# The start of a sliding-window attention kernel: x by halves and row tiles, two GpSimd moves less, one copy on ScalarE

## The chip, the cores and the metric

The kernel runs on one core of a Trainium2 chip. A core has five engines that run side by side and meet only at semaphores: TensorE (PE, matmuls; its weight loads are shown apart as PEld), VectorE (DVE), ScalarE (ACT), GpSimd (POOL) and SyncE (SP), which issues most of the DMAs. The metric is the device time of one execution in microseconds, the median of several runs; less is better.

## The reference

Eight sequences of 32 new positions each attend to a window of 2048 cached positions, 32 query heads over 4 key/value heads.

```python
B, Sq, D = 8, 32, 1024;  Hq, Hkv, Sk, Dh = 32, 4, 8192, 128      # bf16
W = min(4096, max(256, Sk // 4))                                 # 2048
q = (x @ wq).reshape(B, Sq, Hq, Dh).transpose(0, 2, 1, 3)
k = repeat(k_cache[:, :, Sk - W:, :], 8, axis=1)                 # v likewise
p = softmax(einsum("bhqd,bhkd->bhqk", q, k) * Dh ** -0.5)
o = einsum("bhqk,bhkd->bhqd", p, v)
return o.transpose(0, 2, 1, 3).reshape(B, Sq, Hq * Dh) @ wo
```

## The kernel before

The work is cut into 32 units, one for each pair of key/value head g and sequence b, in the order g 0 with b 0 to 7, then g 1, and so on. A unit has 256 queries (8 heads of 32 rows) and 2048 keys in 16 tiles of 128. It runs in four chunks of four key tiles. For a chunk PE computes the scores (L504, four matmuls into `s_ps`, from kT and the projected queries QT), ACT takes the exponential into `pT` (L506), and two chunks later PE multiplies `pT` by V (L515, eight matmuls into `o_ps`; V has a column of ones, which gives the softmax's sum). `s_ps` has two buffers, so the scores of a chunk wait for the exp two chunks before. When a unit is through, `finish_unit` on DVE divides and transposes (L444, L448, L450). The order of instructions on every engine is that of the program text (`manual_schedule`), and `side_plan` puts side work into numbered slots, four to a unit: pieces of the query projections of later heads (`q_pieces`, L285), of the output projection (`o_pieces`, L321), and the preparation of some K tiles.

The scores need K transposed (`kT`), and there are three ways to get it:

- Units 0, 1 and 2: K is loaded as it is (`k_raw`, L192, L197), transposed by PE, and copied out of PSUM by DVE (unit 0: L396, L400; units 1 and 2: `k_pieces`, L244, L246).
- The units of the table `V_T` (4, 7, 9, 12 and so on): K is loaded as it is, DVE transposes 32x32 blocks in four pieces (L259, `kb`), and sixteen moves put the blocks in their places (`kTv`). The last number of a unit's entry says how many of the sixteen go to POOL (L270); the others are DVE's (L268). Unit 9 has 12, so DVE has four, and its moves are spread over the slots 26 to 33; the unit's own scores begin in slot 36.
- All others: a transposing DMA (L200).

V is copied into the `va` buffers (L438 on DVE, L436 on POOL for units 1 and 2). Loads are issued by SP in the order of the text; a load waits on SP for its buffer to come free, and everything behind it on SP waits too.

`start` is what comes ahead of unit 0. x is 256 rows in two row tiles of 128. Tile 0 is loaded by SP (L346), tile 1 by ACT's queue (L347), then SP issues the weights of head group 0 (`wq`, L168, four pieces of one chunk, then one of two, and two of one; a chunk is 128 of the 1024 inputs), with the first half of unit 0's K between (L197). Meanwhile PE runs `N_WARM` matmuls on constants (L374). `x_turn` then transposes x with PE: eight chunks times two row tiles, in two halves of four chunks, each half into one PSUM tile; DVE copies the first two chunks of a half into `xT`, ACT the other two. Then `q_mm` projects (L404): for each of the eight chunks, heads 0 to 3 with all 256 rows and heads 4 to 7 with the 128 rows of tile 0 alone. Rows 128 to 255 of heads 4 to 7 come later in `q_late` (L301, slots 0 to 2 for heads 4 and 5, slots 8 to 12 for heads 6 and 7), two heads at a time, and a copy by DVE (L304) puts them into QT, where unit 4 is the first that reads them.

Of the kernel before, what the change touches and what calls it, by code (L numbers as in the profile page):

```python
# [11 lines left out]
BF16 = mybir.dt.bfloat16  # L12
# [3 lines left out]

RL_LIMIT = 1.0e22
RL_MIN = 1.0e-10
N_WARM = 8
VA_ROW = 160  # L20
V_HALVES = 30

# [1 line left out]

V_T = {4: (None, (4, 6, 6, 7), 8, 15, 9),
       7: (4, (18, 18, 19, 20), 20, 27, 12),
       9: (5, (23, 24, 25, 26), 26, 34, 12),
       **{u: (u - 4, range(4 * u - 14, 4 * u - 10), 4 * u - 11, 4 * u - 2, 12) for u in (12, 14, 17, 19, 22, 24, 27, 29)}}
W_AT = (3, 3, 4, 4, 8, 8, 9, 9, 11, 12, 13, 14, 15, 15, 17, 17, 18, 19, 19, 20, 22, 22, 23, 24, 25, 26, 28, 28)

# [78 lines left out]
class Fast:  # L109
# [183 lines left out]
    def q_late(self, h0):  # L293
        nc, P, DC, B = self.nc, self.P, self.DC, self.B
        st = {}

        def piece(i):
            if i == 0:
                st["ps"] = self.ps_m.tile([P, 2, P], FP32, name="ql_ps", tag="m")
            for c in range(DC):  # L300
                nc.tensor.matmul(st["ps"][:, i, :], lhsT=self.wq_t[0, c // (DC // 2)][:, c % (DC // 2), (h0 + i) * P:(h0 + i + 1) * P],  # L301
                                 rhs=self.xT[:, c, P:self.NQ], start=(c == 0 and i == 0), stop=(c == DC - 1), skip_group_check=True)
            if i == 1:
                nc.vector.tensor_copy(out=self.q_view(0)[:, B // 2:, h0:h0 + 2, :].rearrange("p b h s -> p h b s"),  # L304
                                      in_=st["ps"][:, :, :].rearrange("p h (b s) -> p h b s", b=B // 2))
        return [lambda i=i: piece(i) for i in range(2)]

    def o_pieces(self, g, t, cuts=(512, 512), st=None):
# [29 lines left out]
    def start(self):  # L338
        nc, P = self.nc, self.P
        warm = self.ps_s.tile([P, 512], FP32, name="warm_ps", tag="s_ps")  # L340
        one = nc.const_aps.tensor
        x_sb = self.vp.tile([P, self.NT, self.D], BF16, name="x_sb", tag="v")
        xf = self.x.rearrange("b s d -> (b s) d")
        H = self.DC // 2

        nc.sync.dma_start(out=x_sb[:, 0, :], in_=xf[0:P, :])  # L346
        nc.scalar.dma_start(out=x_sb[:, 1, :], in_=xf[P:2 * P, :])  # L347
        wq0 = self.load_wq(0, 0, (1, 1, 1, 1)) + self.load_wq(0, 1, (2, 1, 1))
        for p in wq0[:5]:
            p()  # L350
        self.load_k(0, 0)
        wq0[5]()
        wq0[6]()
        self.load_k(0, 1)
        self.load_v(0, nc.sync)
        self.load_k(1)
        self.weights = []
        for g in range(self.Hkv):
            if g + 1 < self.Hkv:
                self.weights += self.load_wq(g + 1, 0) + self.load_wq(g + 1, 1)  # L360
            if g:
                self.weights += self.load_wo(2 * g - 2) + self.load_wo(2 * g - 1)
        self.weights += self.load_wo(2 * self.Hkv - 2) + self.load_wo(2 * self.Hkv - 1)
        self.load_v(1, nc.sync)
        self.load_k(2)
        self.load_k(4)
        self.load_v(2, nc.sync)
        self.load_unit(3)
        for v in self.va:
            nc.gpsimd.memset(v[:, :, self.Dh:self.VW], 1.0)  # L370
        nc.gpsimd.memset(self.ones_c[:, :], 1.0)
        def warm_up(n):
            for i in range(n):
                nc.tensor.matmul(warm[:, :], lhsT=one(1.0, [P, P], BF16), rhs=one(1.0, [P, 512], BF16), start=True, stop=True)  # L374
        warm_up(N_WARM)


        def x_turn(half, pl, tag):
            ps = pl.tile([P, H, self.NT, P], BF16, name="xT_ps", tag=tag)
            for c in range(H):  # L380
                for t in range(self.NT):
                    nc.tensor.transpose(ps[:, c, t, :], x_sb[:, t, half * H + c:self.D:self.DC], self.ident[:, :])
            for i, copy in ((0, nc.vector.tensor_copy), (1, nc.scalar.copy)):
                c0 = half * H + i * H // 2
                copy(out=self.xT[:, c0:c0 + H // 2, :], in_=ps[:, i * H // 2:(i + 1) * H // 2, :, :].rearrange("p c t s -> p c (t s)"))

        x_turn(0, self.ps_m, "m")
        x_turn(1, self.ps_s, "s_ps")
        qs = [self.ps_o.tile([P, 2, self.NQ], FP32, name="q0_ps", tag="o_ps") for _ in range(2)]
        qs.append(self.ps_m.tile([P, 4, P], FP32, name="q0_ps", tag="m"))  # L390
        KT = self.KT
        tp = None

        def k_turn(half):
            for j in range(half * KT // 2, (half + 1) * KT // 2):
                nc.tensor.transpose(tp[:, j, :], self.k_raw[0][:, j, :], self.ident[:, :])  # L396

        def k_copy(half):
            sl = slice(half * KT // 2, (half + 1) * KT // 2)
            nc.vector.tensor_copy(out=self.kT[0][:, sl, :], in_=tp[:, sl, :])  # L400

        def q_mm(c, h):
            ps, n = (qs[h // 2][:, h % 2, :], self.NQ) if h < 4 else (qs[2][:, h - 4, :], P)
            nc.tensor.matmul(ps, lhsT=self.wq_t[0, c // H][:, c % H, h * P:(h + 1) * P],  # L404
                             rhs=self.xT[:, c, 0:n], start=(c == 0 and h in (0, 2, 4)), stop=(c == self.DC - 1),
                             skip_group_check=True)

        def q_copy(copy, h0, h1, b0, b1):
            ps = qs[h0 // 2] if h0 < 4 else qs[2]
            copy(out=self.q_view(0)[:, b0:b1, h0:h1, :].rearrange("p b h s -> p h b s"),  # L410
                 in_=ps[:, :, b0 * self.Sq:b1 * self.Sq].rearrange("p h (b s) -> p h b s", s=self.Sq))

        for c in range(self.DC):
            if c == self.DC - 2:
                tp = self.ps_s.tile([P, KT, P], BF16, name="kf_ps", tag="s_ps")
                k_turn(0)
                k_copy(0)
            for h in range(self.rep):
                q_mm(c, h)
            if c == 0:  # L420
                warm_sb = self.c1.tile([P, 8], BF16, name="warm_sb")
                nc.vector.tensor_copy(out=warm_sb[:, :], in_=warm[:, 0:8])
        k_turn(1)
        q_copy(nc.scalar.copy, 0, 2, 0, 1)
        q_copy(nc.vector.tensor_copy, 2, 4, 0, 1)
        q_copy(nc.scalar.copy, 4, 8, 0, 1)
        k_copy(1)
        self.va_copy(0)
        q_copy(nc.vector.tensor_copy, 0, 2, 1, self.B)
        q_copy(nc.vector.tensor_copy, 4, 8, 1, self.B // 2)  # L430
        q_copy(nc.vector.tensor_copy, 2, 4, 1, self.B)
# [262 lines left out]
```

## Time and profile before

| | |
|---|---|
| median of 7 runs | 186.35 us (185.36 to 187.9) |
| the profiled execution | 187.34 us, of which the span is 184.6 us |
| PE busy | 178.8 us (97% of the span) |
| PE weight loads | 152.7 us |
| ACT busy | 136.0 us, of it 128.6 in 128 exps of 1027 ns (L506) |
| DVE busy | 123.8 us |
| POOL busy | 90.8 us, of it 86.0 in 129 moves of 667 ns (L270) |
| DVE's moves (L268) | 47 of 430 ns |
| DMA | 51.72 MB, mean 280 GB/s; 512 KB of K or V take about 6 us from issue to landing |
| TensorE clock granted | 0.999 |

The span is what the profiler recorded from the first to the last instruction; the time of an execution includes what lies around it. A group's "idle before" is the time in which its engine did nothing just ahead of it, with the instruction or DMA that ended the wait behind an arrow. PE's groups overlap by their pipelining, so holes are read from the distance of the starts.

### The profile page before, as it was taken

What the parts mean: (1) busy time and instruction counts of PE and PEld (TensorE: products, weight loads), DVE (VectorE), ACT (ScalarE), POOL (GpSimd) and SP (SyncE); (2) the same over time, 40 slices, a digit from 0 to 9 for tenths busy, and PEclk for the clock granted to TensorE, in tenths of its full rate; (3) what the DMA queues carried; (4) which work ended last, traced back from release to release, by engine and by line L of the source; (5) the groups of instructions that cost most, each with busy time, mean ns of one, the idle gap of its engine ahead of it and who ended that gap; (6) DMA issues with size and microseconds to landing.
All of it is one profiled execution on the core that took longest, in us unless ns stands there. A gap on an engine that the chain in (4) does not pass through costs nothing.

```text
span 184.6 us, 5015 instructions
## 1 busy us (share of the span) xinstructions
PE 178.8 (97%) x2026; PEld 152.7 (83%) x2041; DVE 123.8 (67%) x255; ACT 136.0 (74%) x145; POOL 90.8 (49%) x141
## 2 busy tenths in 40 slices
PE   8999999999999999999999999999999999999994
PEld 3899898999998999988767899987878788888843
DVE  0138699689769786486589667767588987554253
ACT  2218788898899888897786687888787788888800
POOL 2002567069891976916917915929805949600000
PEclk9999999999999999999999999999999999999999
DMA  5999999899999999999999999999999999950003
GB/s 194 330 408 404 211 383 373 260 253 253 365 395 237 353 274 289 373 288 375 232 380 335 402 260 286 355 273 354 277 319 221 364 265 361 218 166 0 0 32 89
DMA packets 52953, 51.72 MB, mean 280 GB/s; under 512 B 39744, under 2 KB 40256, under 8 KB 52928
## 3 DMA queue, kind: packets, MB, share of 16 engines
q1 hardware_dynamic: 52352, 50.90, 97.8%
q10 hardware_dynamic: 576, 0.49, 0.9%
q8 instruction: 15, 0.25, 0.5%
q14 instruction: 10, 0.08, 0.1%
HBM read 41.42 MB, written 0.52 MB: 227 GB/s over the span
## 4 chain that ended last, share of the span: by engine, by line
PE 68%; DMA 12%; DVE 10%; POOL 4%; SPq 2%; issue 2%; POOLq 0%
PE o_ps L515 23%; PE s_ps L504 23%; PE op_ps L321 12%; PE q_ps L285 9%; DMA k_raw<-in_k_cache_dram 9%; POOL kTv L270 4%; DMA v_sb<-in_v_cache_dram 4%; DVE kb L259 3%; DVE kTv L268 2%; DVE o_sb L448 1%; SPq L168 1%; DVE va L438 1%; DVE OT L450 1%; SPq L200 1%; DVE kT L246 1%
## 5 line engine op out<-in xcount | busy, mean ns | idle before, releaser
L506 ACT ACTIVATE pT<-s_ps 128x1024 bf16<-128x1024 f32 x128 | 128.6, 1027 | 29.0 <-PE s_ps L504 28.7
L270 POOL TENSOR_SCALAR kTv<-kb 32x512 bf16<-32x512 bf16 x129 | 86.0, 667 | 51.1 <-DVE kb L259 21.1
L515 PE MATMUL o_ps<-va,pT 128*128 128x129 bf16 x1024 | 78.8, 220 | 0.1
L515 PEld LDWEIGHTS <-pT 128*128 128x128 bf16 x1024 | 68.5, 98 | 3.1
L504 PE MATMUL s_ps<-QT,kT 128*128 128x256 bf16 x336 | 50.4, 273 | 0.5 <-ACT pT L506 0.3
L504 PEld LDWEIGHTS <-kT 128*128 128x128 bf16 x336 | 31.8, 98 | 10.3 <-DMA kT<-in_k_cache_dram 0.7
L321 PE MATMUL op_ps<-wo_sb,OT 128*128 128x512 bf16 (+2 forms) x129 | 32.9, 353 | 0.6
L259 DVE STREAM_TRANSPOSE kb<-k_raw 128x512 bf16<-128x512 bf16 x44 | 29.7, 691 | 2.0 <-DMA k_raw<-in_k_cache_dram 1.7
L285 PE MATMUL q_ps<-xT,wq_sb 128*128 128x256 bf16 x192 | 28.3, 273 | 0.0
L438 DVE COPY va<-v_sb 128x2048 bf16<-128x2048 bf16 x30 | 25.3, 843 | 4.4 <-DMA v_sb<-in_v_cache_dram 3.9
L504 PE MATMUL s_ps<-QT,kTv 128*128 128x256 bf16 x176 | 26.4, 272 | 0.9 <-DVE kTv L268 0.5
L444 DVE RECIPROCAL RL_all<-o_ps 128x2 f32<-128x2 f32 x32 | 5.4, 167 | 28.0 <-PE o_ps L515 27.6
L504 PEld LDWEIGHTS <-kTv 128*128 128x128 bf16 x176 | 16.8, 98 | 7.6 <-issue 1.0
L268 DVE COPY kTv<-kb 32x512 bf16<-32x512 bf16 x47 | 20.2, 430 | 1.1
L285 PEld LDWEIGHTS <-wq_sb 128*128 128x128 bf16 x192 | 16.9, 98 | 1.2
L450 DVE STREAM_TRANSPOSE OT<-o_sb 128x256 bf16<-128x256 bf16 x32 | 14.3, 445 | 1.1
L448 DVE TENSOR_TENSOR o_sb<-o_ps,RL_all 128x256 bf16<-128x256 f32 x32 | 13.6, 424 | 1.1
L321 PEld LDWEIGHTS <-OT 128*128 128x128 bf16 x144 | 11.3, 98 | 2.3
L436 POOL TENSOR_SCALAR va<-v_sb 128x2048 bf16<-128x2048 bf16 x2 | 3.8, 1899 | 17.9 <-DMA v_sb<-in_v_cache_dram 17.9
L288 ACT CAST QT<-q_ps 128x512 bf16<-128x512 f32 x12 | 7.0, 580 | 0.2 <-PE q_ps L285 0.2
L328 DVE TENSOR_TENSOR oacc<-op_ps,oacc 128x512 f32<-128x512 f32 x8 | 5.3, 662 | 2.0 <-PE op_ps L321 2.0
L404 PE MATMUL q_ps<-xT,wq_sb 128*128 128x256 bf16 (+1 forms) x64 | 6.2, 254 | 0.2 <-DMA wq_sb<-in_wq_dram 0.2
(34 smaller groups left out, 43.8 us busy)
## 6 DMA issues: line engine op xcount, KB each, us to landing
v_sb<-in_v_cache_dram SPq DMA_DIRECT2D x30, 512.0 KB, 6.6
wo_sb<-in_wo_dram SPq DMA_DIRECT2D x16, 512.0 KB, 6.5
wq_sb<-in_wq_dram SPq DMA_DIRECT2D x13, 512.0 KB, 6.6
k_raw<-in_k_cache_dram SPq DMA_DIRECT2D x13, 512.0 KB, 5.7
wq_sb<-in_wq_dram SPq DMA_DIRECT2D x6, 256.0 KB, 4.8
v_sb<-in_v_cache_dram SPq DMA_DIRECT2D x4, 256.0 KB, 4.8
kT<-in_k_cache_dram SPq DMA_TRANSPOSE x36, 7.0
k_raw<-in_k_cache_dram SPq DMA_DIRECT2D x2, 256.0 KB, 6.5
```

What stands on the lines that cost most here:

```text
L259: nc.vector.transpose(out=st["kb"][:, sl, :], in_=self.k_raw[ui][:, sl, :])
L268: nc.vector.tensor_copy(out=out, in_=in_)
L270: nc.gpsimd.tensor_scalar(out=out, in0=in_, scalar1=1.0, scalar2=1.0, op0=ALU.mult, op1=ALU.mult)
L285: nc.tensor.matmul(st[k][:, hl % 2, :], lhsT=self.wq_t[g, i][:, c % (DC // 2), hl * P:(hl + 1) * P], rhs=self.xT[:, c, :], start=(c == 0 a ...
L288: nc.scalar.copy(out=self.q_view(g)[:, :, 2 * k:2 * k + 2, :].rearrange("p b h s -> p h b s"), in_=st[k][:, :, :].rearrange("p h (b s) -> ...
L321: nc.tensor.matmul(ps[:, 0:w], lhsT=self.OT[:, gq, c, t * P:(t + 1) * P], rhs=self.wo_t[gq][:, c, n0:n0 + w], start=(k == 0), stop=(k == 7))
L438: self.nc.vector.tensor_copy(out=out, in_=in_)
L448: nc.vector.tensor_tensor(out=o_sb[:, :, :, :], in0=o_ps[:, :, 0:Dh].rearrange("p q (i c) -> p q c i", c=4), in1=rl[:, ui * QT_N:(ui + 1) ...
L450: nc.vector.transpose(out=self.OT[:, g * QT_N:(g + 1) * QT_N, :, b * self.Sq:(b + 1) * self.Sq], in_=o_sb[:, :, :, :])
L504: nc.tensor.matmul(s_ps[:, jj, :], lhsT=self.kT[ui][:, c * CJ + jj, :], rhs=q_u, start=True, stop=True)
L506: nc.scalar.activation(out=pT[:, :, :], in_=s_ps[:, :, :], func=ACT.Exp, bias=0.0, scale=self.scale)
L515: nc.tensor.matmul(o_ps[:, qt, 0:self.VW], lhsT=pT[:, jj, qt * P:(qt + 1) * P], rhs=va[:, j, 0:self.VW], start=(j == 0 and qt == 0), stop= ...
```

## The change

Four things change. The load of x tile 0 is cut into two halves by columns, one issued by SP and one by ACT, ahead of ACT's load of tile 1; one warm-up matmul is left out (8 to 7). `x_turn` takes a row tile instead of a half of the chunks: eight transposes of tile 0 into one PSUM tile, eight of tile 1 into the other; DVE copies chunks 0 to 3 of a row tile and ACT chunks 4 to 7, and in chunk 0 the projection takes heads 4 to 7 first. Unit 9 gives 10 moves to POOL instead of 12, and 6 to DVE. The copy of the second `q_late` group (heads 6 and 7) is made by ACT instead of DVE; it stands behind the eleventh exp and ahead of the twelfth.

```diff
--- before.py
+++ after.py
@@ -16,7 +16,7 @@
 
 RL_LIMIT = 1.0e22
 RL_MIN = 1.0e-10
-N_WARM = 8
+N_WARM = 7
 VA_ROW = 160
 V_HALVES = 30
 
@@ -24,7 +24,7 @@
 
 V_T = {4: (None, (4, 6, 6, 7), 8, 15, 9),
        7: (4, (18, 18, 19, 20), 20, 27, 12),
-       9: (5, (23, 24, 25, 26), 26, 34, 12),
+       9: (5, (23, 24, 25, 26), 26, 34, 10),
        **{u: (u - 4, range(4 * u - 14, 4 * u - 10), 4 * u - 11, 4 * u - 2, 12) for u in (12, 14, 17, 19, 22, 24, 27, 29)}}
 W_AT = (3, 3, 4, 4, 8, 8, 9, 9, 11, 12, 13, 14, 15, 15, 17, 17, 18, 19, 19, 20, 22, 22, 23, 24, 25, 26, 28, 28)
 
@@ -301,8 +301,9 @@
                 nc.tensor.matmul(st["ps"][:, i, :], lhsT=self.wq_t[0, c // (DC // 2)][:, c % (DC // 2), (h0 + i) * P:(h0 + i + 1) * P],
                                  rhs=self.xT[:, c, P:self.NQ], start=(c == 0 and i == 0), stop=(c == DC - 1), skip_group_check=True)
             if i == 1:
-                nc.vector.tensor_copy(out=self.q_view(0)[:, B // 2:, h0:h0 + 2, :].rearrange("p b h s -> p h b s"),
-                                      in_=st["ps"][:, :, :].rearrange("p h (b s) -> p h b s", b=B // 2))
+                copy = nc.vector.tensor_copy if h0 == 4 else nc.scalar.copy
+                copy(out=self.q_view(0)[:, B // 2:, h0:h0 + 2, :].rearrange("p b h s -> p h b s"),
+                     in_=st["ps"][:, :, :].rearrange("p h (b s) -> p h b s", b=B // 2))
         return [lambda i=i: piece(i) for i in range(2)]
 
     def o_pieces(self, g, t, cuts=(512, 512), st=None):
@@ -343,7 +344,8 @@
         xf = self.x.rearrange("b s d -> (b s) d")
         H = self.DC // 2
 
-        nc.sync.dma_start(out=x_sb[:, 0, :], in_=xf[0:P, :])
+        for eng, d0 in ((nc.sync, 0), (nc.scalar, self.D // 2)):
+            eng.dma_start(out=x_sb[:, 0, d0:d0 + self.D // 2], in_=xf[0:P, d0:d0 + self.D // 2])
         nc.scalar.dma_start(out=x_sb[:, 1, :], in_=xf[P:2 * P, :])
         wq0 = self.load_wq(0, 0, (1, 1, 1, 1)) + self.load_wq(0, 1, (2, 1, 1))
         for p in wq0[:5]:
@@ -375,14 +377,12 @@
         warm_up(N_WARM)
 
 
-        def x_turn(half, pl, tag):
-            ps = pl.tile([P, H, self.NT, P], BF16, name="xT_ps", tag=tag)
-            for c in range(H):
-                for t in range(self.NT):
-                    nc.tensor.transpose(ps[:, c, t, :], x_sb[:, t, half * H + c:self.D:self.DC], self.ident[:, :])
-            for i, copy in ((0, nc.vector.tensor_copy), (1, nc.scalar.copy)):
-                c0 = half * H + i * H // 2
-                copy(out=self.xT[:, c0:c0 + H // 2, :], in_=ps[:, i * H // 2:(i + 1) * H // 2, :, :].rearrange("p c t s -> p c (t s)"))
+        def x_turn(t, pl, tag):
+            ps = pl.tile([P, self.DC, P], BF16, name="xT_ps", tag=tag)
+            for c in range(self.DC):
+                nc.tensor.transpose(ps[:, c, :], x_sb[:, t, c:self.D:self.DC], self.ident[:, :])
+            for c0, copy in ((0, nc.vector.tensor_copy), (H, nc.scalar.copy)):
+                copy(out=self.xT[:, c0:c0 + H, t * P:(t + 1) * P], in_=ps[:, c0:c0 + H, :])
 
         x_turn(0, self.ps_m, "m")
         x_turn(1, self.ps_s, "s_ps")
@@ -415,7 +415,7 @@
                 tp = self.ps_s.tile([P, KT, P], BF16, name="kf_ps", tag="s_ps")
                 k_turn(0)
                 k_copy(0)
-            for h in range(self.rep):
+            for h in (4, 5, 6, 7, 0, 1, 2, 3) if c == 0 else range(self.rep):
                 q_mm(c, h)
             if c == 0:
                 warm_sb = self.c1.tile([P, 8], BF16, name="warm_sb")
```

## The prediction

> **What bounds the kernel now.** I read the page first: PE is busy 178.8 of 184.6 us, so the order of matmuls fills the span and only holes between them can be won. I then listed the PE timeline and compared the distance between neighbouring groups with their own length (four L504 score matmuls 0.44 us, eight L515 matmuls 0.45 us, four L285 matmuls 0.44 us). Behind the start there are five holes: before the scores of unit 2 (22.31 us, 0.42 lost), unit 4 (31.53, 0.30), unit 9 (55.87, 0.31), unit 16 (91.23, 0.33) and unit 17 (97.23, 0.71). From there to 173 us PE has none worth naming. The chain that ended last, in order of time, tells what each hole hangs on:
>
> ```profile
> 3.55 6.46 DMA k_raw<-in_k_cache_dram
> 10.03 9.93 DMA k_raw<-in_k_cache_dram
> 19.97 0.71 DVE kb L259
> ...
> 30.77 0.63 DVE kTv L268
> 31.53 0.60 PE s_ps L504 x4
> ...
> 55.15 0.67 POOL kTv L270
> 55.87 0.61 PE s_ps L504 x4
> ...
> 84.91 1.16 SPq L200
> 86.17 6.47 DMA v_sb<-in_v_cache_dram
> 92.66 0.89 DVE va L438
> ```
>
> To 20 us the chain is two DMAs, not the projection: the first half of unit 0's K lands at 10.03, its landing lets SP issue unit 4's K, and that lands at 19.97. DVE has the block transpose L259 of that K ahead of unit 0's finish and of unit 2's kT copy (L246), so all three stand behind the DMA. Then it is DVE's row of work up to unit 4, POOL's moves up to unit 9, and at 84.91 a load that SP could issue only when PE had freed a buffer. The timeline of the start:
>
> ```profile
> 4.20 1.75 PEld L382 LDWEIGHTS <-x_sb 128*128 128x128 bf16 x16 [0.76 <-DMA x_sb<-in_x_dram]
> 6.00 3.18 PE L404 MATMUL q_ps<-xT,wq_sb 128*128 128x256 bf16 x32
> 9.38 1.49 PE L404 MATMUL q_ps<-xT,wq_sb 128*128 128x256 bf16 x16 [0.20 <-DMA wq_sb<-in_wq_dram]
> ```
>
> PE is through projection chunks 0 to 3 at about 9.0 and waits until 9.37 for the weights of chunk 4.
>
> **Start: x in halves, transposes by row tile, heads 4 to 7 first, one warm-up matmul less.** The eight warm-ups take 3.57 us; one is 0.43, so seven end near 3.92. Tile 0 (landed at 4.15 by its row, 0.75 + 3.4) now comes from both queues ahead of tile 1. Tile 1 is issued one ACT issue later (0.40), so by its old 3.6 us it lands at 4.75. Eight transposes at the row's 0.109 (1.75/16) take 0.87: tile 0's from 3.92 to 4.79, tile 1's to 5.66; with x no sooner than 4.15 they end at 5.89. Heads 4 to 7 of chunk 0 need only tile 0's copies, and PE starts the projection at 5.7 to 5.9 instead of 6.00: at most 0.33 earlier. I cost this gain at nothing: what covers it is the chunk 4 weight DMA (9.37), and behind that unit 4's K (19.97). If that cover were gone it would be worth 0.33. The four xT copies keep their sizes (0.42 DVE, 0.59 ACT) and ACT's table load moves 0.4 later, with ACT idle until 5.85.
>
> One issue more also shifts SP. SP's own waits (L168 on x_sb 0.3 us, L197 on wq_sb 2.0) fit the built instruction stream: each DMA waits for the landing of the one eight issues before it, ACT's issues counted. With three x DMAs instead of two, the first K half, issued at 3.55 without a wait, now waits for the first half of x tile 0; the later loads keep their predecessors. That half is 128 KB of the 512 KB that landed by 4.35. I take it as landed by 3.5 (the DMA timeline shows the first bytes at 1.8 us and 350 GB/s by 3 us, so 256 KB are moved by about 2.8), which costs nothing; the other end is 4.20, the old landing, 0.65 later.
>
> Rows of 1 KB instead of 2 KB make 128 packets more, 8 on each of 16 engines. Between 83 and 84 us the queue moved 895 packets, nearly all small, in 1 us: 16/895 = 18 ns each. So 0 to 0.14 us; I take 0.05, on the path through unit 4's K.
>
> The Trainium skill speaks against the split ("DMA: Bandwidth & Descriptors", "Issuing engines are not separate DMA queues"): issues from several engines run on the same 16 DMA engines and save only issue time. By it tile 0 comes no sooner than 4.15 and the start gains 0.1 rather than 0.33; covered either way.
>
> **Second late projection copy from DVE to ScalarE.** Around unit 4:
>
> ```profile
> 24.80 6.44 POOL L270 TENSOR_SCALAR kTv<-kb 32x512 bf16<-32x512 bf16 x9 [1.55 <-PE o_ps L515]
> 26.58 3.77 ACT L506 ACTIVATE pT<-s_ps 128x1024 bf16<-128x1024 f32 x4 [0.29 <-PE s_ps L504]
> 27.23 0.40 DVE L304 CAST QT<-ql_ps 128x256 bf16<-128x256 f32 x1
> 30.46 0.92 DVE L268 COPY kTv<-kb 32x512 bf16<-32x512 bf16 x2
> 31.50 0.34 PEld L504 LDWEIGHTS <-kTv 128*128 128x128 bf16 x4 [0.40 <-POOL kTv L270]
> ```
>
> DVE runs without a pause from L304 to its last move at 31.38 (its RECIPROCAL at 29.34 could start at 28.9, as PE's o_ps is done by 28.72). Without L304 DVE ends 0.40 earlier, at 30.98. But POOL's nine moves end at 31.24 all the same: with the 0.05 from POOL's end to PE's start seen at unit 9 (55.82 to 55.87), the scores can start at 31.29. PE itself gets there at 31.23 (30.79 + 0.44). On ACT the copy stands behind the eleventh exp (ends 26.30) and ahead of the twelfth; ACT's copies of 64, 128 and 512 columns (0.21, 0.27, 0.58) put 256 columns at 0.37. The gap before the twelfth exp is 0.29, so the exps, and PE's next score groups, which start right after the exp that frees their bank, come up to 0.09 late; PE's own time becomes 31.32. Gain 31.53 - 31.32 = 0.21. Bounds: 0.30 if ACT's copy overlaps its neighbours, 0 if the copy's whole 0.37 falls on the exps.
>
> **Unit 9: ten GpSimd moves instead of twelve.**
>
> ```profile
> 47.05 8.77 POOL L270 TENSOR_SCALAR kTv<-kb 32x512 bf16<-32x512 bf16 x12 [0.45 <-DVE kb L259]
> 49.43 0.17 DVE L444 RECIPROCAL RL_all<-o_ps 128x2 f32<-128x2 f32 x1 [1.21 <-PE o_ps L515]
> 53.93 0.17 DVE L444 RECIPROCAL RL_all<-o_ps 128x2 f32<-128x2 f32 x1 [1.33 <-PE o_ps L515]
> 55.05 0.29 DVE L268 COPY kTv<-kb 32x512 bf16<-32x512 bf16 x1
> ```
>
> A POOL move is 8.77/12 = 0.73; ten end 1.46 earlier, at 54.4. DVE gets two moves more, of 0.29 to 0.66. In the new order one stands before each of the two RECIPROCALs, in idle gaps of 1.21 and 1.33 us, so they are hidden; without that cover they would push unit 6's and unit 7's finish by up to 1.3. DVE's last move still ends at 55.34, so with the 0.15 from DVE's end to PE seen at unit 4 the scores may start at 55.49, while PE gets there at 55.56: DVE is next, 0.07 behind. The gain is 0.31, less the exps: between 51.9 and 55 PE's groups follow at 0.92, not 0.89, because ACT holds them, and without the hole that goes on for the two or three groups before the next projection piece (0.06). I take 0.25; 0 if DVE's last move takes 0.66.
>
> **After that.** PE is 0.46 earlier at 56 us. It keeps this if the holes at 91.23 and 97.23 move too. SP's waits on PE (13 us between 40 and 80) and the chain at 84.91 say so: the load behind unit 17's hole is issued when PE frees the kT buffer, and the DMA queue was nearly empty before its data (about 20 GB/s around 89 us). Sum: -0.21 - 0.25 + 0.05 = -0.41. The profiled execution took 187.34 us (span 184.6 and 2.7 around it), so 186.9; it lay 1 us above the median of the runs, so the median goes from 186.35 to 185.9.
>
> **Rivals.** (A) The start counts as well: chunk 4's weights and unit 4's K land sooner as tile 0's and the weight pieces' issues move up. For it: DMA rate dips to 246 GB/s at 4.4 us. Against it: the bytes ahead of both are the same. 185.9 - 0.33 = 185.6. (B) The gain is given back at 97.23 because transfers and not buffers decide there. For it: the DMA share is near 1 through the middle. Against: the nearly empty queue. 186.35 + 0.05 = 186.4. (C) Slower: the first K half waits for x's first half. If that lands after 3.55, the head of the chain shifts by the difference, unit 4's K and unit 2's scores with it: up to 185.9 + 0.65 = 186.6. (D) Slower: PE's full rate comes later. The 512-column warm-ups follow at 0.43 us and the same width later (L321) at 0.22; PE's count per 0.2 us doubles at about 6.7 us, though the granted clock column shows 1.00 throughout. With a shorter warm-up the change may come later. Half rate costs nothing until about 7.5 (chunks 0 to 3 need 2.6 us at full rate out of the 3.5 before 9.37). A delay of one warm-up (3.57, to 10.3) puts chunk 4 at 10.7, 1.3 late; unit 2's hole swallows 0.42, and unit 4's goes whole (PE there at 32.2, 0.7 late). 0.7 - 0.25 + 0.05 gives 186.85.
>
> The skill's "TensorE: Matmul & The Clock Gate" (Part 1) has the rate double after a free-running window of 3.4 us spent busy; the warm-ups alone would fill 3.0 us of one instead of 3.4, so (D) would be decided by whether transposes follow without a pause, and would cost about the same.
>
> **How the numbers follow.** Forecast 0.50, (A) 0.11, (B) 0.13, (C) 0.12, (D) 0.10, others 0.04. The range takes the largest gains (0.30 + 0.31 + 0.33: 185.4) and the price of (D), 186.9, and 0.3 below and 0.1 above for a median whose runs spread over 2.5 us: 185.1 to 187.0. A difference under 1% (1.9 us) can hardly be told from none here, and no case reaches it alone; I leave 0.04 for faster and 0.08 for slower, the latter for (C) and (D) together.
>
> **What would show it.** Right: PE starts the projection near 5.7 and still waits at chunk 4 until about 9.4; unit 2's hole stays at 22.3; unit 4's scores come at about 31.3 and unit 9's hole is gone, with POOL's ten moves done by 54.5; unit 17 starts near 96.8. Wrong: k_raw's first issue later than 3.6, PE's rate doubling after 7.5, an ACT gap in PE's groups between 26.8 and 28.6, DVE's unit 9 moves as the last wait before unit 9, or unit 17 still at 97.2.

## The result and the profile after

The median after is 185.85 us (184.92 to 186.99, 26 runs); beside it the kernel before took 185.95 us (184.67 to 188.07, 63 runs). The ratio is 0.9997 with a 95% interval of 0.9981 to 1.0013, that is -0.06 us with an interval of -0.35 to +0.24. No difference was measured. Here and below the ratios and the mean spans leave out the few runs that took over 1.5% longer than the fastest of their kernel; the medians have all runs. The profiled execution took 186.32 us with a span of 184.5.

The forecast of 185.9 is met by luck and not for its reasons. It was 0.45 below a median of seven runs that itself lay 0.4 above the larger series; the predicted gain of 0.41 lies outside the measured interval. Of the two gains, unit 9's came at unit 9 (whether it lasts to the end is not shown) and the copy's did not come at all. And the change pays 0.45 us at a place that the prediction did not look at: the last half microsecond.

The page of the profile after (here and below the fences show chosen rows of a view):

```profile
span 184.5 us, 5015 instructions
PE 178.0 (96%) x2025; PEld 152.6 (83%) x2040; DVE 124.6 (68%) x256; ACT 136.1 (74%) x146; POOL 89.8 (49%) x139
L270 POOL TENSOR_SCALAR kTv<-kb 32x512 bf16<-32x512 bf16 x127 | 85.1, 670 | 51.4 <-DVE kb L259 26.0
L268 DVE COPY kTv<-kb 32x512 bf16<-32x512 bf16 x49 | 22.2, 452 | 1.2
```

POOL has two moves less (127), DVE two more (49). The span is 184.54 against 184.56, though PE's last matmul ends at 181.38 instead of 181.85: what PE gained in this profile is gone again behind it.

The chain of waits after (start, length, what):

```profile
3.08 6.46 DMA wq_sb<-in_wq_dram
9.59 1.49 PE q_ps L404 x16
...
31.70 0.60 PE s_ps L504 x4
...
55.89 0.46 PE s_ps L504 x4
...
85.03 6.61 DMA v_sb<-in_v_cache_dram
91.65 1.12 DVE va L438
...
96.75 0.60 PE s_ps L504 x4
```

At the start the chain is still a DMA (now chunk 4's weights). At unit 4 it now stays on PE, but only just: by the profile PE is through at 31.57 and DVE's last move at 31.55. Unit 9's first scores no longer end a wait: the piece at 55.89 is only one of a row that follows at 0.92 us. From 85 us the chain is again the load of a V and DVE's row behind it, without the 1.16 us that SP took before it issued that load in before.

The start in the timeline after:

```profile
3.59 0.43 SPq L197 DMA_DIRECT2D k_raw<-in_k_cache_dram  x1
3.61 0.92 PEld L383 LDWEIGHTS <-x_sb 128*128 128x128 bf16 x8 [0.59 <-DMA x_sb<-in_x_dram]
4.89 0.82 PEld L383 LDWEIGHTS <-x_sb 128*128 128x128 bf16 x8 [0.36 <-DMA x_sb<-in_x_dram]
5.76 0.42 PE L404 MATMUL q_ps<-xT,wq_sb 128*128 128x128 bf16 x4
6.48 2.58 PE L404 MATMUL q_ps<-xT,wq_sb 128*128 128x256 bf16 x28 [0.29 <-DVE xT L385]
9.59 1.49 PE L404 MATMUL q_ps<-xT,wq_sb 128*128 128x256 bf16 x16 [0.53 <-DMA wq_sb<-in_wq_dram]
```

Tile 0's halves landed at 3.39 and 3.57 and tile 1 at 4.85 (before, tile 0 at 4.16 and tile 1 at 4.34). Tile 0's transposes begin at 3.61 and tile 1's at 4.89 (4.20 for both before). The projection starts at 5.76 with heads 4 to 7, and heads 0 to 3 wait for tile 1's copy until 6.48. Then PE stands 0.53 before chunk 4, whose weights are no sooner (9.54 for 9.33).

Around unit 4, after:

```profile
24.98 6.42 POOL L270 TENSOR_SCALAR kTv<-kb 32x512 bf16<-32x512 bf16 x9 [1.58 <-PE o_ps L515]
26.36 0.38 ACT L305 CAST QT<-ql_ps 128x256 bf16<-128x256 f32 x1
26.76 3.77 ACT L506 ACTIVATE pT<-s_ps 128x1024 bf16<-128x1024 f32 x4
27.20 2.28 DVE L268 COPY kTv<-kb 32x512 bf16<-32x512 bf16 x4
29.51 0.17 DVE L444 RECIPROCAL RL_all<-o_ps 128x2 f32<-128x2 f32 x1
30.63 0.92 DVE L268 COPY kTv<-kb 32x512 bf16<-32x512 bf16 x2
31.66 0.35 PEld L504 LDWEIGHTS <-kTv 128*128 128x128 bf16 x4 [0.38 <-POOL kTv L270]
```

Before, DVE's three moves behind the copy and its RECIPROCAL were:

```profile
27.65 1.66 DVE L268 COPY kTv<-kb 32x512 bf16<-32x512 bf16 x3
29.34 0.17 DVE L444 RECIPROCAL RL_all<-o_ps 128x2 f32<-128x2 f32 x1
```

The copy is ACT's (0.38) and gone from DVE, but from DVE's second move to its RECIPROCAL there are 2.31 us (27.20 to 29.51) against 2.32 before (27.02 to 29.34). The hole before unit 4 is 0.29, against 0.30.

Unit 9, after:

```profile
47.22 7.35 POOL L270 TENSOR_SCALAR kTv<-kb 32x512 bf16<-32x512 bf16 x10 [0.45 <-DVE kb L259]
48.41 0.58 DVE L268 COPY kTv<-kb 32x512 bf16<-32x512 bf16 x1
49.59 0.17 DVE L444 RECIPROCAL RL_all<-o_ps 128x2 f32<-128x2 f32 x1 [0.60 <-PE o_ps L515]
52.78 0.58 DVE L268 COPY kTv<-kb 32x512 bf16<-32x512 bf16 x1
54.09 0.17 DVE L444 RECIPROCAL RL_all<-o_ps 128x2 f32<-128x2 f32 x1 [0.73 <-PE o_ps L515]
55.76 0.60 PE L504 MATMUL s_ps<-QT,kTv 128*128 128x256 bf16 x4
```

Ten moves end at 54.57. The two new DVE moves lie in the gaps before the RECIPROCALs, which shrink from 1.21 to 0.60 and from 1.33 to 0.73. The scores at 55.76 wait for no move.

### The profile page after: what moved, and what is told of

Same layout as the page of the kernel before. It is cut to its first block, busy times and chain, and to the rows that moved or that the text cites. A ratio compares the mean times of both kernels' runs of the same rounds, so it can differ in the third digit from the quotient of the medians.

```text
span 184.5 us, 5015 instructions
## 1 busy us (share of the span) xinstructions
PE 178.0 (96%) x2025; PEld 152.6 (83%) x2040; DVE 124.6 (68%) x256; ACT 136.1 (74%) x146; POOL 89.8 (49%) x139
## 4 chain that ended last, share of the span: by engine, by line
PE 86%; DMA 7%; DVE 3%; SPq 1%; issue 1%; ACT 1%; ACTq 0%
PE s_ps L504 29%; PE o_ps L515 29%; PE op_ps L322 12%; PE q_ps L285 11%; DMA v_sb<-in_v_cache_dram 4%; DMA wq_sb<-in_wq_dram 4%; PE q_ps L404 2%; PE ql_ps L301 1%; SPq L168 1%; PE tp L244 1%; DVE kb L259 1%; DVE va L438 1%; ACT pT L506 1%; PE kf_ps L396 0%; DVE kTv L268 0%
## 5 line engine op out<-in xcount | busy, mean ns | idle before, releaser
L270 POOL TENSOR_SCALAR kTv<-kb 32x512 bf16<-32x512 bf16 x127 | 85.1, 670 | 51.4 <-DVE kb L259 26.0
L438 DVE COPY va<-v_sb 128x2048 bf16<-128x2048 bf16 x30 | 24.7, 823 | 3.2 <-DMA v_sb<-in_v_cache_dram 2.8
L268 DVE COPY kTv<-kb 32x512 bf16<-32x512 bf16 x49 | 22.2, 452 | 1.2
L404 PE MATMUL q_ps<-xT,wq_sb 128*128 128x128 bf16 (+1 forms) x64 | 6.0, 246 | 0.8 <-DMA wq_sb<-in_wq_dram 0.5
```

The lines of the kernel that those rows point to most:

```text
L268: nc.vector.tensor_copy(out=out, in_=in_)
L270: nc.gpsimd.tensor_scalar(out=out, in0=in_, scalar1=1.0, scalar2=1.0, op0=ALU.mult, op1=ALU.mult)
L438: self.nc.vector.tensor_copy(out=out, in_=in_)
```

## The experiments

"Before" is run beside each group of kernels; its medians there were 185.91, 185.99 and 185.99 us. The time outside the span varies from 1.7 to 3.0 us between executions, so sizes of 0.2 to 0.5 are read from the traces and the times say whether they agree. There is one trace of each kernel, fourteen with before and after. The diffs show the lines that matter; the rest is left out.

| kernel | median us | ratio to before, 95% |
|---|---|---|
| start_only | 186.39 | 1.0014 [0.9983, 1.0044] |
| copy_only | 185.79 | 0.997 [0.9942, 0.9998] |
| unit9_only | 185.71 | 0.9967 [0.9938, 0.9996] |
| no_split | 185.70 | 0.999 [0.9962, 1.0018] |
| unit4_early | 186.56 | 1.0023 [0.9996, 1.0051] |
| old_start_early | 185.67 | 0.9979 [0.9945, 1.0012] |
| before_one_more | 186.47 | 1.0024 [1.0003, 1.0044] |
| after_one_less | 185.69 | 0.998 [0.9958, 1.0002] |
| early_one_less | 185.96 | 0.9988 [0.9959, 1.0016] |
| copy_twice, unit4_dve, before_two_more | 185.46, 186.91, 186.42 | one execution each |

### The parts one by one

**start_only**: the change without its unit 9 and copy parts.

```diff
# against after
-       9: (5, (23, 24, 25, 26), 26, 34, 10),
+       9: (5, (23, 24, 25, 26), 26, 34, 12),
-                copy = nc.vector.tensor_copy if h0 == 4 else nc.scalar.copy
+                copy = nc.vector.tensor_copy
```

> Only the start of the change (x in column halves, seven warm-ups, transposes by row tile, heads 4 to 7 first); unit 9 and the late copy as before. Theory: the start buys nothing, since PE waits for chunk 4's weights, and the split of x delays the DMA stream: chunk 4 starts near 9.6 us and unit 2's scores near 22.5, as in the changed kernel (9.59 and 22.49), against 9.38 and 22.31 before; everything behind is 0.2 late. Rival: the 0.2 is the jitter of one profile; chunk 4 then starts anywhere from 9.3 to 9.6 and unit 2 with it. Time: ratio 1.000 to 1.002.

**copy_only** and **unit9_only**: one part alone, put into the kernel before.

```diff
# copy_only, against before
+                copy = nc.vector.tensor_copy if h0 == 4 else nc.scalar.copy
# unit9_only, against before
-       9: (5, (23, 24, 25, 26), 26, 34, 12),
+       9: (5, (23, 24, 25, 26), 26, 34, 10),
```

> Only the second late projection copy on ScalarE. Theory: DVE's moves of unit 4 wait for POOL's, move by move (0.64 to 0.66 us against 0.28 free), and the copy from PSUM had filled one such wait, so its removal frees nothing: DVE's last move stays at 31.4 and unit 4's scores at 31.5, ratio 1.000. Rival, the prediction's step: unit 4's scores come 0.2 earlier, at 31.3, ratio 0.999.

> Only unit 9 with 10 moves on GpSimd. Theory: the hole of 0.31 us before unit 9 closes, 0.25 of it stays as a gain: unit 9's scores at 55.6 instead of 55.87, and unit 17's at 97.0 or earlier; ratio 0.9985. Rival: transfers take it back at unit 17 (97.2), ratio 1.000.

**no_split**: the change with x tile 0 in one load.

```diff
# against after
-        for eng, d0 in ((nc.sync, 0), (nc.scalar, self.D // 2)):
-            eng.dma_start(out=x_sb[:, 0, d0:d0 + self.D // 2], in_=xf[0:P, d0:d0 + self.D // 2])
+        nc.sync.dma_start(out=x_sb[:, 0, :], in_=xf[0:P, :])
```

> The changed kernel with x tile 0 in one load of 2 KB rows on SP again, all else as changed. Theory: without the 1 KB rows and the third x load the DMA stream is as before: chunk 4 starts at 9.4 and unit 2's scores at 22.3, 0.2 earlier than in the changed kernel, so the gain of unit 9 shows: ratio 0.9985. Rival: the order of the transposes or the shorter warm-up is what delays, and chunk 4 stays at 9.6.

Unit 9's part works as far as unit 9. From unit 7's first scores to unit 9's there are 8.86 to 8.88 us in the seven kernels with twelve moves and 8.58 or 8.59 in the seven with ten: 0.28 less. (unit9_only's first scores were expected at 55.6 and came at 55.90, since a wait of 0.39 stood before unit 7 in that execution.)

How much of the 0.28 reaches the end is not shown. From unit 17's first scores to PE's last matmul there are 84.62 or 84.63 us in all fourteen profiles, so a gain must show at unit 17, and those scores start anywhere from 96.07 to 97.23: on average at 96.45 with ten moves and at 96.74 with twelve, but with ranges that overlap (96.07 to 96.92 and 96.31 to 97.23). In time unit9_only is 0.33% below before; so is copy_only (0.30%), which has twelve moves.

The idea that the split delays chunk 4 falls. The group of chunk 4 starts at 9.38 in before and 9.59 in after, but at 9.30 in start_only, where 9.6 was expected, and at 9.50 in no_split, where 9.4 was (unit 2's scores at 22.44 there, expected 22.3). The five profiles with the split have 9.10 to 9.61, the nine without it 9.13 to 10.45. Unit 4's K lands at 19.95 in before and 20.13 in after; with the split it lands from 19.03 to 20.13, without it from 19.30 to 20.08. The split and the unsplit starts are not apart in either.

### Why the copy brings nothing

**copy_twice** issues the DVE copy of heads 6 and 7 twice; **unit4_dve** gives all sixteen moves of unit 4 to DVE.

```diff
# copy_twice, against before
+                for _ in range(1 if h0 == 4 else 2):
# unit4_dve, against before
-V_T = {4: (None, (4, 6, 6, 7), 8, 15, 9),
+V_T = {4: (None, (4, 6, 6, 7), 8, 15, 0),
```

> The kernel before with the second late projection copy made twice by DVE, at the same place. Theory: DVE's moves go one to each POOL move, so DVE's time from the first to the end of the fourth move (2.31 us with the copy among them and without it) grows by a whole POOL period, 0.67, to about 2.98. Rival: DVE's work simply adds up, +0.40, to 2.72.

> The kernel before with all sixteen moves of unit 4 on DVE and none on POOL. Theory (POOL's moves are what DVE's wait for): each of the sixteen takes 0.28 us. Rival (a move is slow for another reason, its bank of partitions or the transposes before it): a good part still takes 0.6. Unit 4's scores come later either way, by about 1.5 us, since DVE has nine moves more.

The groups of L268 from 24 to 32.2 us (durations min/median/max in ns, first and last start), in this order before, after, copy_twice and unit4_dve:

```profile
L268 DVE COPY kTv<-kb x7: 281/315/661, 24.7 to 30.8; 32x512 bf16<-32x512 bf16 x7
```

```profile
L268 DVE COPY kTv<-kb x7: 281/617/661, 24.9 to 30.9; 32x512 bf16<-32x512 bf16 x7
```

```profile
L268 DVE COPY kTv<-kb x7: 283/290/664, 24.4 to 31.1; 32x512 bf16<-32x512 bf16 x7
```

```profile
L268 DVE COPY kTv<-kb x16: 282/285/291, 24.2 to 31.9; 32x512 bf16<-32x512 bf16 x16
```

With POOL silent no move is slow (unit 4's scores came 12.77 us after its K landed, for 11.58 in before: 1.2 later, where 1.5 was expected). Beside POOL a DVE move takes 0.28 when it comes first and up to 0.66 when it has to sit out a POOL move (0.67 here), so while both have moves to make they go one to one. The copy out of PSUM does not take part: it is 0.40 beside POOL and 0.40 in unit4_dve, where POOL has no moves. In before it therefore ran inside a wait that DVE's next move had to make anyway. That move took 0.32 behind the copy; without the copy it takes 0.64. The median of the group goes from 315 to 617 for this reason, with no more work in it.

The second copy is no longer free. Timeline of copy_twice:

```profile
26.90 0.86 DVE L305 CAST QT<-ql_ps 128x256 bf16<-128x256 f32 x2
27.78 1.87 DVE L268 COPY kTv<-kb 32x512 bf16<-32x512 bf16 x3
29.68 0.17 DVE L445 RECIPROCAL RL_all<-o_ps 128x2 f32<-128x2 f32 x1
```

From the second move (26.69) to the RECIPROCAL it is 2.99 (expected 2.98), 0.67 more than before: one whole POOL move for 0.43 of copy. Over the whole row the price is smaller. From the first block transpose of unit 4's K to the end of DVE's last move there are 11.41 us in before, 11.40 in after, start_only, copy_only and after_one_less, 11.39 in unit9_only, 12.07 in copy_twice and 12.69 in unit4_dve. But of copy_twice's 0.66 more, 0.31 lies ahead of the copy, between the first and the second block transpose, where DVE had to wait for PE. From the second transpose on it is 9.55 against 9.20, 0.35 more: DVE's last move comes when POOL is done (30.86) and takes 0.29, where in before it sat out a POOL move and took 0.62. Removing the copy is worth 0.01 us.

The Trainium skill says the same of the mechanism ("SBUF — State Buffer", "Who interferes with whom"): a DVE copy in a two-port mode and a GpSimd instruction hold a shared pair of ports for a whole instruction, and the second waits for all of it. The rows above agree in the wait (0.28 alone, up to 0.66 behind a POOL move); the ports themselves no trace shows. The first section's "meet only at semaphores" is therefore too strong: DVE's moves follow one another at 0.01 us here, and the wait is spent inside the move.

By its trace copy_only should equal before, yet it timed at 0.997, its interval just short of 1. Its profile shows no shorter row; that this is the scatter of the runs is not shown. Its first scores of unit 4 did come at 31.14, sooner than the rival's 31.3 and without a hole before them. But unit 4's K had landed at 19.49, 0.46 sooner than in before, so DVE's row of the same length ended at 30.91, and unit 2 had not waited, so PE came later than DVE. before_two_more, with the copy on DVE, shows nearly the same: K at 19.67, scores at 31.24, a hole of 0.05.

### Closing unit 4's hole

The sixteen moves of unit 4 could be spread over two slots less, which is meant to take the wait away by the order rather than by the copy. **unit4_early** does it in after, **old_start_early** in before with the copy and unit 9 parts, **early_one_less** is unit4_early with one DMA less (the next part tells why).

```diff
# unit4_early, against after (early_one_less: also V_HALVES = 31)
-V_T = {4: (None, (4, 6, 6, 7), 8, 15, 9),
+V_T = {4: (None, (4, 6, 6, 7), 8, 13, 9),
# old_start_early, against before: the same line, the copy by nc.scalar.copy, unit 9 with 10
```

> The changed kernel with unit 4's moves spread over slots 8 to 12 instead of 8 to 14, so that DVE's last two stand ahead of unit 2's finish. Theory: DVE's last move no longer waits for POOL's last; unit 4's scores follow POOL's end by 0.05, 4.25 us behind DVE's second move instead of 4.50, and the hole before unit 4 shrinks from 0.29 to 0.05; ratio to the kernel before 0.998. Rival: unit 2's later finish or its output buffer holds PE elsewhere and unit 9 starts no sooner; ratio 0.9995.

> The kernel before with unit 9's ten moves, the late copy on ScalarE and unit 4's moves in slots 8 to 12; x and the start as before. Theory: the start's edits are worth nothing, so this does as well as the changed kernel with unit 4's moves early: ratio 0.998. Rival: the start's edits cost some 0.2 us, and this is faster by that: 0.997.

> The changed kernel with unit 4's moves in slots 8 to 12 and unit 30's V in one load. Theory: both holes (units 4 and 9) are closed and the end is 2.71 us: ratio 0.997. Rival: with PE 0.3 earlier the holes before units 7 and 17 grow (as in the profile with the early moves alone) and take it back: 0.998.

DVE's row is shorter in all three: from the second block transpose to the last move's end it takes 8.47 to 8.49 us, against 9.20 in before. No hole stands before unit 4, and from unit 2's first scores to unit 4's there are 8.90 us, against 9.22 in before and 9.21 in after. But these profiles do not show that the order closed it. In all three unit 2 had not waited, so PE came to unit 4 after POOL's end and 4.31 to 4.58 us behind DVE's second move (expected 4.25); copy_only and before_two_more, also without a wait at unit 2 but with the old slots, have 8.90 and 8.95.

The time does not follow either. In unit4_early PE is 1.2 ahead of after at unit 4, as the K landed 1.1 sooner, and meets the next wait at unit 7. Its timeline:

```profile
36.57 0.69 DVE L438 COPY va<-v_sb 128x2048 bf16<-128x2048 bf16 x1 [0.76 <-DMA v_sb<-in_v_cache_dram]
38.03 10.06 POOL L270 TENSOR_SCALAR kTv<-kb 32x512 bf16<-32x512 bf16 x14 [7.77 <-PE o_ps L515]
46.44 0.61 PE L504 MATMUL s_ps<-QT,kTv 128*128 128x256 bf16 x4 [0.29 <-POOL kTv L270]
```

V lands when it lands, DVE's copy waits 0.76 for it with the last block piece of unit 7 behind, and POOL's long row of moves ends too late for PE. The same group waits 0.48 in early_one_less and not at all in old_start_early. The three times lie on both sides of 1, so no gain of this step is measured.

### The missing half microsecond

start_only's median is 0.5 above before's (its interval still has 1 in it), though in its profile PE's last matmul ends at 181.36 against 181.85. From PE's last matmul to the span's end the records give 2.71 us in before, copy_only, unit9_only and no_split, and 3.16 or 3.17 in after, start_only and unit4_early. So far only kernels with the split have it. What SP waits for from 176 us on, first before, then after (us in total, times, longest):

```profile
core 0 of [0], span 184.6 us
SPq L689 <- DMA out_dram<-o_t: 1.0, 3, 0.4
```

```profile
core 0 of [0], span 184.5 us
SPq L689 <- DMA out_dram<-o_t: 1.6, 1, 1.6
```

Before, SP waits three times, a little each; after, once, for long. The times of SP's eight last checks and of the last output's landing, in us after PE's last matmul, from the records:

```
before  last out landed 1.83; checks 0.29 0.36 0.42 0.49 0.84 1.23 1.41 1.83
after   last out landed 1.83; checks 1.84 1.91 1.98 2.05 2.11 2.17 2.23 2.29
```

The records give each DMA a semaphore, and there are eight of them in rotation. Before has 128 DMAs, sixteen rounds of eight; after has 129. In before the last output DMA is on the semaphore that SP checks last; the split adds one DMA, every later one moves on by one, and the last output is now on the one that is checked first. SP stands there until 1.84 and has seven checks left at 0.065 each: 0.45.

The rival is that x's second queue itself costs something at the end. It is told apart by DMAs that have nothing to do with x. V of the units from `V_HALVES` on is loaded in two DMAs instead of one, so 29 adds one DMA, 28 adds two, and 31 takes one away.

```diff
# before_one_more: 29, before_two_more: 28 (against before); after_one_less: 31 (against after)
-V_HALVES = 30
+V_HALVES = 29
```

> The kernel before with one DMA more, far from the start: unit 29's V is loaded in two halves, as unit 30's and 31's are. Theory: the eight completion counters are used in turn, so one DMA more puts the last output DMA on the counter that SP checks first at the end, and the seven other checks (0.065 us each) come after its landing: from PE's last matmul to the end of the span 3.16 us instead of 2.71, ratio 1.0024. Rival: the longer end belongs to x's second queue or to the start, and the end stays at 2.71, ratio 1.000.

> The kernel before with two DMAs more (V of units 28 and 29 in halves). Theory: the last output DMA is on the counter that SP checks second, six checks come after it: 2.71 + 6 x 0.065 = 3.10 us from PE's last matmul to the end. Rival: any further DMA adds the same again, 3.6, or none does, 2.71.

> The changed kernel with one DMA less: unit 30's V in one load instead of two, so that the last output DMA is again on the counter checked last. Theory: the end is 2.71 us again, 0.45 less than in the changed kernel, and the gain of unit 9 shows in the time: ratio to the kernel before 0.998. Rival: the later landing of unit 30's V delays its copy, or the time does not follow the span: ratio 1.000.

SP's waits at the end in before_one_more, then in after_one_less:

```profile
core 0 of [0], span 184.1 us
SPq L689 <- DMA out_dram<-o_t: 1.6, 1, 1.6
```

```profile
core 0 of [0], span 184.0 us
SPq L689 <- DMA out_dram<-o_t: 0.8, 2, 0.6
```

From PE's last matmul to the end it is 3.16 in before_one_more, 3.10 in before_two_more (the last output on the second check, so six to come), 2.70 in after_one_less and 2.80 in early_one_less (0.09 of it behind the last check). x tile 0 has one load in the first two and two in the others, so the rival falls. (old_start_early has 4.50: in its one profile an output landed 3.6 after PE, which no other shows.) In time, before_one_more is 1.0024 [1.0003, 1.0044], which is 0.45 us. after_one_less at 0.998 is 0.0017 below after, 0.3 us, but the intervals of the two overlap. The spans, which the record has for every run and which leave out what lies around them, are clearer: on average before_one_more's is 0.53 us above before's (interval 0.24 to 0.81) and after_one_less's 0.52 below after's (0.17 to 0.88). The latter two were not run side by side, but before's mean span was 183.77 to 183.86 in each of the three groups of runs.

## Why the prediction was right, and where it was wrong

- **Start, costed at nothing: right.** The projection began at 5.76 (forecast 5.7 to 5.9) and waited for chunk 4 as before. That it began in the forecast's 0.2 us is partly luck: the four other profiles with the split have 5.49 to 6.15, the nine without it 5.64 to 6.24. Tile 0 landed at 3.39 and 3.57, earlier than in no_split (4.07) although the skill's rule on issuing engines, as the prediction applied it, had it no sooner than 4.15. But tile 1 landed at 4.85 (4.85 to 5.55 in the five profiles), later than the forecast's 4.75 and before's 4.34, so all of x was there no sooner and heads 0 to 3 began at 6.48 instead of 6.00. The 0.5 to 0.7 of tile 0 bought nothing, since the cover held.
- **1 KB rows, +0.05: not separable.** Unit 4's K lands between 19.0 and 20.1 in the fourteen profiles, with no sign of the split.
- **Copy, -0.21: wrong.** The step that failed is "Without L304 DVE ends 0.40 earlier, at 30.98": it ended at 31.55, as unit 4's K landed 0.18 later than before and the row behind it was as long to 0.01. ACT's side was right (0.38 for 0.37). The profile had the reason in it: three moves behind the copy took 1.66, not 0.84, because of POOL, and a row whose pace another engine sets does not shrink by the length of one member.
- **Unit 9, -0.25: right up to unit 9.** 0.28 less from unit 7 to unit 9, POOL done at 54.57 for 54.4, both new moves hidden in the named gaps, PE then following at 0.92 us as the forecast had it for PE held by the exps. That PE keeps it to the end is not shown.
- **The end, not in the sum: +0.45.** The prediction counted the rotation of eight only for what SP waits for when it issues a load, where it was right ("the later loads keep their predecessors"), and did not follow it to the last DMA.
- **Sum.** Read from the traces it is -0.28 + 0 + 0.45 = +0.17 if unit 9's part is kept, within the measured -0.35 to +0.24.

Of the rivals, (A) falls: the start paid nothing. (B) stays open. Unit 17's first scores come at 96.75 after for 97.23 before, as forecast, but start_only, with twelve moves, has 96.73. In before's profile SP stood until 86.07 in the issue of a transposing load and issued unit 17's V at 86.17; in the thirteen others that V was issued at 84.58 to 85.81. So these 0.48 cannot be put down to unit 9. The hole before unit 17 is from 0 to 1.0 us in the fourteen profiles, more than any part of the change is worth, and why is open. (C) came, but small: the first K half shares a semaphore with the half of x tile 0 from ACT's queue, which landed at 3.57, and was issued at 3.59 instead of 3.55 (in unit4_early 3.64 and 3.65). (D) falls: 128-column matmuls follow at 0.056 us by 5.9 us, so PE's full rate was there sooner than in before (about 6.7). The moment varies, from 4.0 to 6.6 in the six profiles with seven warm-ups and from 4.6 to 6.8 in the eight with eight, always before the 7.5 up to which the prediction had it cost nothing.

No kernel here is faster beyond doubt. unit9_only is the best measured (0.9967), but copy_only, whose trace gives no reason for it, is as good within the intervals. The sum says that the part worth trying alone is unit 9's, with the number of DMAs left as it was.

## What to carry to other kernels

An engine whose instructions must take turns with a neighbour's is paced by that neighbour: ask what its row takes as a whole before subtracting an instruction from it, since an instruction that takes no part in the turns may have been running in a wait. When a change adds or takes away a DMA, follow the count to the kernel's last transfer as well as to the loads behind it. And when a forecast hits, compare the change and not only the end value, since a median of a few runs can lie as far off as the whole gain.

## What the runs showed of the hardware

Where the last output DMA stands in the rotation of eight semaphores moves the end by up to 0.45 us (2.71 with it checked last, 3.10 second, 3.16 first, from PE's last matmul to the end), with the same work and the same landing time. A DVE move beside GpSimd takes 0.28 or up to 0.66 by who comes first, while a copy out of PSUM takes 0.40 either way. Split over two queues, with tile 1 behind it on ACT's, the 256 KB of x tile 0 were there at 3.52 to 3.64 us in five profiles, against 4.02 to 4.50 in nine as one load with tile 1 beside it; tile 1 landed later in exchange, at 4.85 to 5.55 for 4.21 to 4.68.
